# Two sets of halves of q and k, freer order of scores and transposes, in an attention and MLP kernel

## The chip, the cores and the metric

The kernel runs on one core of one Trainium2 chip. The metric is the device time of one execution, in microseconds (us). Three runs of the kernel before took 924.66, 919.51 and 918.96 us, a median of 919.51. The engines are named as in the profile: PE is TensorE (PEld its weight loads), DVE is VectorE, ACT is ScalarE, POOL is GpSimd, SP is SyncE, whose queue (SPq) issues nearly all transfers.

## The reference

Causal attention in blocks of 64 over q, k and v of shape (8 batches, 8 heads, 576, 64), and on its result, reshaped to 4608 tokens of 512, an MLP with 2048 hidden units and the activation h * tanh(softplus(h)):

```python
scores = scale * np.matmul(q, k.transpose(0, 1, 3, 2))
scores = np.where(block_i >= block_j, scores, -1000000000.0)   # blocks of 64
scores = scores - np.max(scores, axis=-1, keepdims=True)
attn = np.exp(scores)
attn = attn / (np.sum(attn, axis=-1, keepdims=True) + 1e-09)
out = np.matmul(attn, v)                # attention
...
h = x @ w_in                            # (4608, 512) @ (512, 2048)
sp = np.where(h > 20.0, h, np.log1p(np.exp(np.minimum(h, 20.0))))
y = (h * np.tanh(sp)) @ w_out           # (4608, 2048) @ (2048, 512)
```

All inputs and outputs are f32.

## The kernel before

Most products are made of pairs of f16 numbers: a matrix is split into a high half (the value in f16) and a low half (the rest), and a product is three matmuls, high by high, high by low, low by high. Scales that are powers of two, found from sums of squares, keep the halves in range.

The work is in tiles of 512 tokens. Tile b holds tokens of batch b, for b from 0 to 7; a ninth tile holds the 64 tokens that each batch has over 512. A tile has three stages: attention of the batch by pairs of heads (4 pairs), m1 (x by w_in, with the activation behind it) and m2 (by w_out, then the store). Attention of batch 0 has a form of its own (`attend`, L1345 to L1493, in f32). Batch 1 takes the scores in f32, and batches 2 to 7, 24 pairs, take them from halves (`attend_pair`). m1 is plain for the first tiles (L2156), then a scheme of seven products in place of eight (L2247); m2 is plain (L2596) up to tile 6 and by seven products after that (L2428). Attention of batch b runs beside m1 and m2 of the tile before it, so that PE always has matmuls that need nothing new.

A pair of batches 2 to 7 goes as follows. `load_pair` issues the loads of q and k into the f32 rooms `qf` and `kl`, and of v. ACT takes the sums of squares of both (L1173), and as it must write its squares somewhere, it writes them into the low halves QL and KL. A small matmul (L779) adds over the partitions, DVE makes the scales (L757, L767, L1185). Then the high halves QH and KH are made on ACT (L1213), DVE (L1217) or POOL (L792), and the low halves on DVE (L1225). There is one set of these four halves, so the squares of a pair must wait until PE has taken the scores of the pair before it (`wait_s`, with NQ = 1). The scores are three rounds in two banks of PSUM (`ss_ring`): L1563 for the products, each a pair of 64-row matmuls for the two heads of the pair, and L1575 for the columns that lie outside the mask: `far_q` times `far_k`, a constant tile of 64 columns of 2^120, adds a very large negative number. DVE takes the maxima (L1609 to L1619), ACT the exponentials (L1645), which are split in halves into a ring of three tiles P (cast on any of three engines, L1689; subtraction on DVE or POOL, L1696). SP transposes each by DMA into a ring of four tiles PT (L1724, and L1739 for a late piece). PE multiplies with v (L1779), DVE divides (L1845, L1846).

The program is a list of operations, each with what it needs (`after`), which ring rooms it takes and frees, and on which engines it can run. `Plan.order` lays them out with a table of due times, `AT` (one number for each operation), and a string, `WAY`, that names the engine of each operation that has a choice. In each engine the operations stand in the order so found, and each engine works strictly through its own list. The operations are given to the planner pair by pair. Besides the real needs two chains of needs are given: `last["S"]`, by which each round of scores comes after the round before it, over all pairs, and `last["T"]`, by which each transpose comes after the one before it.

Other lines that the prediction speaks of: the weight w_in comes in eight pieces of 1 MB (L853), each put together from its parts by a cast (L876) on ACT, DVE or POOL and an operation of DVE (L891); `far_q` columns for batch 0 (L1357, L1431); subtraction of the maxima for batch 0 on PE (L1459), which needs a scaled unit matrix from ACT (L810); casts of k and q for the maxima (`kr`, `qr`: L1297 on ACT, L1303 on DVE, L1308 on POOL); the exponentials of batch 0 (L1477); the activation (L2184 in the plain m1, L2300 in the other); the factors of the output (L1057) and the scaled output on ACT (L2637).

Of the kernel before, what the change touches and what calls it, by code (L numbers as in the profile page):

```python
# [12 lines left out]
BF16 = mybir.dt.bfloat16  # L13
F32 = mybir.dt.float32
# [7 lines left out]
P = 128  # L22
# [7 lines left out]
FULL = 1  # L30
EARLY = 6
SEVEN = 7
NWORK, NOT, NQ, NV, NPT, NP2 = 3, 1, 1, 1, 4, 3
# [2911 lines left out]
```

## Time and profile before

| what | value |
|---|---|
| median of three runs | 919.51 us (918.96 to 924.66) |
| profiled execution | 919.17 us, span of its instructions 917.4 us |
| PE, PEld busy | 908.8 us (99%), 636.6 us (69%) |
| DVE, ACT, POOL busy | 775.8 us (85%), 610.5 us (67%), 254.9 us (28%) |
| mean granted clock of PE | 1.000 |
| transfers | 129.94 MB, 142 GB/s |
| chain that ended last | PE 85%, DVE 6%, DMA 4%, ACT 2% |

The profile comes from the execution of 919.17 us. Busy time of an engine is the time in which at least one of its instructions runs; a PE instruction is shown up to the modelled end of its pipeline, so that consecutive matmuls overlap and their starts, not their lengths, tell the rate. In square brackets stands the idle time of the engine before an instruction, with what ended it. The chain of waits is followed back from the last instruction to what released each.

### The profile page before, as it was taken

The numbers are of one execution on the slowest core, as the hardware profiler recorded it, in microseconds if no ns is written. First come the engines' busy times: TensorE is split into PE (matmuls) and PEld (weight loads), VectorE is DVE, ScalarE is ACT, GpSimd is POOL, SyncE is SP. The second block draws the span as 40 slices with busy tenths as digits, with TensorE's granted clock in tenths as the row PEclk, the third lists the DMA queues.
The fourth block names the chain that finished last, engine by engine and source line by source line (L and its number), as shares of the span: only waits on it lengthen the run. The fifth ranks groups of instructions, "written<-read, shape, count | busy, mean of one in ns | idle before, by whom it ended". The sixth has DMA issues, their size and how long they took to land.

```text
span 917.4 us, 22914 instructions
## 1 busy us (share of the span) xinstructions
PE 908.8 (99%) x9288; PEld 636.6 (69%) x9288; DVE 775.8 (85%) x1466; ACT 610.5 (67%) x1043; POOL 254.9 (28%) x245
## 2 busy tenths in 40 slices
PE   8999999999999999999999999999999999999998
PEld 6976765555557865687557855785578757888887
DVE  6989999999989898698888887789778898984871
ACT  4789998799657974587569855677478433652540
POOL 2101221512245053343223341312614112300310
PEclk9999999999999999999999999999999999999999
DMA  9876997756798778867796588776877450015001
GB/s 304 263 227 155 214 242 158 142 125 153 153 192 175 150 145 181 157 128 152 156 200 140 110 176 176 162 135 125 178 135 138 77 112 14 1 52 111 2 1 47
DMA packets 298154, 129.94 MB, mean 142 GB/s; under 512 B 250944, under 2 KB 279616, under 8 KB 298048
## 3 DMA queue, kind: packets, MB, share of 16 engines
q1 hardware_dynamic: 297616, 128.16, 64.5%
q8 instruction: 72, 1.18, 0.5%
q10 hardware_dynamic: 432, 0.33, 0.1%
q14 instruction: 34, 0.28, 0.1%
HBM read 58.06 MB, written 10.49 MB: 75 GB/s over the span
## 4 chain that ended last, share of the span: by engine, by line
PE 85%; DVE 6%; DMA 4%; ACT 2%; SPq 1%; issue 1%; POOL 1%; DVEq 0%; POOLq 0%; ACTq 0%
PE acc L2247 28%; PE acc L2596 27%; PE ss L2428 8%; PE acc L2156 7%; PE ss L1563 7%; PE acc L1779 7%; DMA wo_l<-in_w_in_dram 2%; DVE P L1696 1%; DVE pv L1609 1%; DVE PT L1387 1%; DMA sx<-in_v_dram 1%; PE acc L1493 1%; DVE Gt L891 1%; DMA many<-in_k_dram 1%; DMA PT<-P 0%
## 5 line engine op out<-in xcount | busy, mean ns | idle before, releaser
L2596 PE MATMUL acc<-Gt,wo_h 128*128 128x512 f16 x896 | 266.7, 379 | 0.0
L2596 PE MATMUL acc<-Gt,wo_l 128*128 128x512 f16 x448 | 169.8, 379 | 0.0
L1645 ACT ACTIVATE pe<-ss,pv 128x192 f32<-128x192 f32 (+2 forms) x240 | 126.7, 608 | 60.5 <-DVE pv L1619 44.2
L2247 PE MATMUL acc<-x,wi_h 128*128 128x256 f16 x896 | 151.1, 273 | 0.0
L2596 PEld LDWEIGHTS <-wo_h 128*128 128x128 f16 x896 | 81.5, 98 | 86.1 <-issue 3.8
L2247 PE MATMUL acc<-x,wi_l 128*128 128x256 f16 x448 | 122.1, 273 | 0.0
L2247 PE MATMUL acc<-x,sx 128*128 128x256 f16 x1008 | 120.9, 273 | 0.0
L1609 DVE TENSOR_REDUCE pv<-ss 128x2 f32<-128x384 f32 (+4 forms) x140 | 104.5, 788 | 16.2 <-PE ss L1575 15.9
L2247 PEld LDWEIGHTS <-sx 128*128 128x128 f16 x1008 | 97.8, 98 | 14.4 <-issue 0.8
L2105 DVE SCALAR_TENSOR_TENSOR Gt<-F,bv,Gt 128x1024 f16<-128x1024 f32 (+2 forms) x80 | 95.4, 1203 | 3.5 <-POOL Gt L792 2.2
L2247 PEld LDWEIGHTS <-wi_h 128*128 128x128 f16 x896 | 86.3, 98 | 15.1 <-issue 1.1
L1696 POOL TENSOR_TENSOR P<-pe,P 128x256 f16<-128x256 f32 (+3 forms) x58 | 70.5, 1237 | 82.5 <-DVE P L1689 30.9
L2156 PE MATMUL acc<-x,wi_h 128*128 128x384 f16 (+2 forms) x384 | 80.5, 308 | 0.6 <-ACT F L2184 0.6
L2596 PEld LDWEIGHTS <-wo_l 128*128 128x128 f16 x448 | 43.8, 98 | 53.0
L1779 PEld LDWEIGHTS <-PT 128*128 128x128 f16 x2128 | 72.0, 97 | 9.2 <-issue 0.4
L2300 ACT ACTIVATE F<-acc,bv 128x512 f32<-128x512 f32 x84 | 57.0, 683 | 31.9 <-PE acc L2247 31.8
L1696 DVE TENSOR_TENSOR P<-pe,P 128x256 f16<-128x256 f32 (+3 forms) x110 | 73.9, 714 | 1.8 <-POOL P L1689 0.9
L1779 PE MATMUL acc<-many,PT 128*128 128x65 f16 (+1 forms) x2128 | 74.2, 193 | 0.0
L1563 PE MATMUL ss<-many 64*128 64x64 f16 (+7 forms) x1280 | 73.7, 260 | 0.0
L1689 POOL CAST P<-pe 128x256 f16<-128x256 f32 (+3 forms) x55 | 38.1, 717 | 90.8 <-ACT pe L1645 49.2
L2156 PE MATMUL acc<-x,wi_l 128*128 128x384 f16 (+2 forms) x192 | 56.0, 308 | 0.0
L1563 PEld LDWEIGHTS <-many 64*128 64x128 f16 x1152 | 33.6, 94 | 29.1 <-issue 14.8
(254 smaller groups left out, 1650.1 us busy)
## 6 DMA issues: line engine op xcount, KB each, us to landing
sx<-in_w_out_dram SPq DMA_DIRECT2D x16, 511.8 KB, 4.4
many<-in_v_dram SPq DMA_DIRECT2D x28, 288.0 KB, 3.2
many<-in_k_dram SPq DMA_DIRECT2D x28, 288.0 KB, 3.5
many<-in_q_dram SPq DMA_DIRECT2D x28, 256.0 KB, 3.5
out_dram<-ot SPq DMA_DIRECT2D x28, 256.0 KB, 2.8
wo_l<-in_w_in_dram SPq DMA_DIRECT2D x6, 1023.8 KB, 8.0
many<-in_v_dram SPq DMA_DIRECT2D x28, 192.0 KB, 3.4
many<-in_v_dram SPq DMA_DIRECT2D x28, 96.0 KB, 3.0
```

Of the source, the lines that this page charges most:

```text
L1563: nc.tensor.matmul(ss[:, 512 * a + col : 512 * a + col + n], lhsT=m[q_][hs, at : at + P], rhs=m[k_][hs, key : key + n], start=first, stop= ...
L1609: nc.vector.reduce_max(out=mx[:, c], in_=ss[:, :, c0:c1], axis=mybir.AxisListType.X)
L1645: nc.scalar.activation(pe[ex[r].slot][:, cols], ss_[S0[r].slot][:, cols], AF.Exp, scale=esc, bias=mx[:, c, a : a + 1],)
L1689: op(out=h, in_=x)
L1696: eng.tensor_sub(l, x, h)
L1779: nc.tensor.matmul(out, lhsT=p_, rhs=v_, start=first, stop=True, skip_group_check=True,)
L2105: nc.vector.scalar_tensor_tensor(out=dst[:, 1], in0=src, scalar=self.s_g, in1=dst[:, 0], op0=ALU.mult, op1=ALU.subtract,)
L2156: nc.tensor.matmul(pt, lhsT=w[:, d, f * P : (f + 1) * P], rhs=rhs(x, d), start=k == 0 and d == 0 and z == 0, stop=d == NP - 1 and z == 2, ...
L2247: nc.tensor.matmul(pt[:, k * TH : (k + 1) * TH], lhsT=weights(kind, z, d, k), rhs=x_[:, d, blk, x, :], start=first and k == 0 and d == 0 a ...
L2300: lambda: nc.scalar.activation(dst(), src(), AF.Mish, scale=scale),
L2428: nc.tensor.matmul(pt[:, k * TH : (k + 1) * TH], lhsT=weights(kind, z, s, c, k), rhs=block(blk, x, s, c), start=one, stop=s == NS - 1 and ...
L2596: nc.tensor.matmul(pt, lhsT=w[:, f, o * P : (o + 1) * P], rhs=g, start=s == 0 and c == 0 and z == 0, stop=s == NS - 1 and c == FG - 1 and ...
```

## The change

- There are two sets of halves QH, QL, KH, KL (`sets`, NQ = 2). Pair i of batches 1 to 7 uses set (i + 1) mod 2, and its squares and halves wait for the scores of the pair two before it, not one. The f32 rooms `qf` and `kl` stay single. The second set lies at the end of the tile `many`, which grows from 5632 to 6790 columns.
- To make room, small tiles are joined into one tile `small` (total, far_scale, pv, wv, dv), and `far_k` is no longer a tile of 64 columns: it is one column of `consts`, which the matmul reads 64 times (a broadcast).
- The chain of scores is given only for the first two of the pairs; later ones are ordered within a pair alone. The chain of transposes is gone (L1724 needs only its halves; the late piece L1739 still comes after its own).
- `AT` and `WAY` are new: another order on every engine, and other engines for many operations. No operation is added or removed but for the fills of constants.

```diff
-NWORK, NOT, NQ, NV, NPT, NP2 = 3, 1, 1, 1, 4, 3
+NWORK, NOT, NQ, NV, NPT, NP2 = 3, 1, 2, 1, 4, 3
 AT = (
-    0, 6736, 0, 475, 7565, 3975, 3325, 950, 1425, 10650, 4450, 2375, 1900, 5100, 5750, 6657, 8719,
...
+    0, 1050, 0, 475, 8745, 2850, 3325, 950, 1425, 1900, 5100, 3975, 2375, 8270, 10170, 9695, 7464,
...
 WAY = (
-    "dpdpaaaaaadaaaaadaaadadddppddapadapaaaaaaadppaaaddddadadaaadaaaaapapddaaaapddaaaddadddpdad"
+    "dddpaaaaaappaaaaaappdppaapdddpddaadaapddadpppadpddpdadadaaddaaaaadaapaadpaapaaaapapddpdad"
...
-    many = const.tile([P, 5632], F32, name="many")
+    many = const.tile([P, 5510 + 2 * S + P], F32, name="many")
...
+    small = const.tile([P, NPV * 19 + 2 * 33 + B // 2 + 1], F32, name="small")
...
+    def halves_in(q, k):
+        m = {}
+        for x, t in (("Q", q), ("K", k)):
+            t_ = t.rearrange("p (z n) -> p z n", z=2)
+            m.update({x + "H": t_[:, 0], x + "L": t_[:, 1], x + "F": t.bitcast(F32)})
+        return m
+
+    other = many_h[:, 11020 : 11020 + 4 * S + 2 * P]
+    sets = [
+        halves_in(qk[:, 2 * (S + P) : 4 * (S + P)], qk[:, 4 * (S + P) + 2 * S :]),
+        halves_in(other[:, 0 : 2 * (S + P)], other[:, 2 * (S + P) :]),
+    ]
...
-    far_k = const.tile([P, 64], BF16, name="far_k")
+    far_k = consts.bitcast(BF16)[:, 4:5]
     nc.vector.memset(far_k, 2.0**120)
+    far_k = far_k.to_broadcast([P, 64])
...
-        m = {**(fulls[i % 2] if full else sets[i % NQ]), **v_sets[i % NV]}
+        m = {**(fulls[i % 2] if full else sets[(i + 1) % NQ]), **v_sets[i % NV]}
...
-                S0.append(add("pe", (0.01, 0.0), lambda: None, [last.get("S")], take=[ss_ring]))
-                last["S"] = S0[r]
+                first = [last.get("S")] if len(used) < 2 else []
+                S0.append(add("pe", (0.01, 0.0), lambda: None, first + S0[-1:], take=[ss_ring]))
...
-                [lo, last.get("T")],
+                [lo],
                 take=[pt_ring],
                 free=[(p2_ring, hi)],
             )
-            last["T"] = tr
...
-            back = 2 if b <= FULL else NQ
-            wait_s = used[-back]["S"] if len(used) >= back else []
+            wait_s = used[-2]["S"] if len(used) >= 2 else []
```

How the new tables move instructions is shown at three places. In the changed program the lines are 4 to 5 higher (L1349 for L1345, L1463 for L1459, L814 for L810, L880 for L876, L1481 for L1477; 2 to 4 in the later ones: L1177 for L1173, L2186 for L2184, L1649 for L1645).

Place one, the start of the program. On ACT before, from its third row on (kr and qr are the casts of k and q of pair 1, PT is written with the scaled unit matrix):

```order
L1297 ACT_TABLE_LOAD
L1297 CAST kr_145<-sx_76 128x576
L1297 CAST qr_149<-sx_76 128x384
L810 ACTIVATE PT_107<-P_103 128x128
L1477 ACTIVATE pe_127<-ss_129 128x2x384
L1477 ACTIVATE pe_126<-ss_128 128x2x384
```

and in the change:

```order
L814 ACT_TABLE_LOAD
L814 ACTIVATE PT_105<-P_101 128x128
L1481 ACTIVATE pe_116<-ss_118 128x2x384
L1481 ACTIVATE pe_117<-ss_119 128x2x384
L1301 CAST kr_136<-wo_h 128x576
L1021 ACTIVATE P_100,bv_112<-sx_75 128x640
```

The unit matrix is first now, and the casts of pair 1 stand on POOL. On PE at the same place, before, where the scores of pair 0 end:

```order
L1431 LDWEIGHTS PT_107
L1431 MATMUL ss_129<-far_k,PT_107 128x64
L1459 LDWEIGHTS PT_106
L1459 MATMUL ss_129<-PT_107,PT_106 128x128
L1459 LDWEIGHTS PT_106
```

and in the change:

```order
L1435 LDWEIGHTS PT_105
L1435 MATMUL ss_119<-consts,PT_105 128x64
L1349 MATMUL acc_120<-kr_135,qr_139 128x384
L1349 MATMUL acc_121<-kr_135,qr_139 128x384
L1349 MATMUL acc_120<-kr_135,qr_139 128x128
```

The twelve subtractions L1459 stood right behind the scores; now the maxima products of pair 1 come between.

Place two, the last pieces of w_in. On ACT before (the cast of a piece, then the exponentials of batch 0):

```order
L1819 ACTIVATE dv_124<-acc_131,bv_118 128x4
L876 CAST Gt<-wo_l 128x1024
L1477 ACTIVATE pe_127<-ss_128 128x2x384
L1876 CAST P_102<-many 128x128
L876 CAST wo_l<-sx_76 128x8x64
```

and in the change on POOL:

```order
L880 CAST Gt<-x 128x1024
L1312 CAST qr_138<-wo_h 128x256
L1883 CAST x<-many 128x384 x3
L880 CAST Gt<-wo_l 128x1024 x2
L2828 MEMSET wo_l 128x8x64 x2
```

The last two casts of pieces into Gt have gone to POOL, and no exponential stands behind them.

Place three, m1 of tile 1. On ACT before (squares of q and k of the third pair of batch 2, then a load of the activation's table and two activations):

```order
L1645 ACTIVATE pe_126<-ss_128,pv_116 128x64
L1173 ACTIVATE many,pv_117<-many 128x576 x2
L2184 ACT_TABLE_LOAD
L2184 ACTIVATE F_65<-acc_130,bv_119 128x512
L2184 ACTIVATE F_65<-acc_132,bv_119 128x512
```

and in the change:

```order
L2186 ACT_TABLE_LOAD
L2186 ACTIVATE F_65<-acc_122,bv_113 128x512
L2186 ACTIVATE F_65<-acc_120,bv_113 128x512
L1177 ACTIVATE many,small<-many 128x576
L2095 ACTIVATE Gt<-F_65,bv_113 128x1024
```

One of the two squares has moved behind the two activations, the other stands well ahead of them.

## Rows read from the trace of the kernel before

**Rows 1.** The page, first part: busy time, share and instructions of each engine.
```profile
PE 908.8 (99%) x9288; PEld 636.6 (69%) x9288; DVE 775.8 (85%) x1466; ACT 610.5 (67%) x1043; POOL 254.9 (28%) x245
```

**Rows 2.** Stretches: length, busy PE, PEld, DVE, ACT, POOL, PE's clock, DMA share, GB/s.
```profile
0.00:20.00 20.00, 17.17 (x170) 12.87 (x170) 11.24 (x52) 9.81 (x19) 3.92 (x12) 1.00 0.91 286
900.00:920.00 20.00, 13.50 (x124) 11.84 (x122) 1.79 (x4) 1.31 (x3) 0.00 (x0) 0.99 0.16 53
```

**Rows 3.** Timeline, first 14 us: start, length, instruction, [idle before it, releaser].
```profile
7.56 0.67 ACT L1297 CAST kr<-sx 128x576 fp32r<-128x576 f32 x1 [4.61 <-DMA sx<-in_k_dram]
8.55 0.30 ACT L810 ACTIVATE PT<-P 128x128 f16<-128x128 f32 x1
8.91 0.83 PE L1459 MATMUL ss<-PT,PT 128*128 128x128 f16 x12 [1.69 <-ACT PT L810]
9.67 0.51 PE L1345 MATMUL acc<-kr,qr 64*128 64x384 f32 x4
...
13.03 0.51 POOL L1308 CAST qr<-wo_h 128x384 fp32r<-128x384 f32 x1 [9.90 <-DMA wo_h<-in_q_dram]
```

**Rows 4.** Timeline, 54 to 57 us.
```profile
54.13 1.35 ACT L876 CAST Gt<-wo_l 128x1024 f16<-128x1024 bf16 x1 [2.16 <-DMA wo_l<-in_w_in_dram]
...
56.20 1.09 PE L1420 MATMUL ss<-wo_h 64*128 64x192 f32 x12 [0.91 <-ACT pe L1477]
```

**Rows 5.** Timeline, 153 to 157 us.
```profile
153.17 2.34 DVE L970 SCALAR_TENSOR_TENSOR wo_l<-sx,wo_s,wo_h 128x2048 f16<-128x2048 f32 x1
...
155.68 0.69 ACT L2637 ACTIVATE ot<-acc,bv 128x512 f32<-128x512 f32 x1 [2.49 <-DVE bv L1057]
...
156.42 0.16 PE L779 MATMUL acc<-bv,consts 128*128 128x4 bf16 x1 [0.35 <-ACT ot L2637]
```

**Rows 6.** Timeline, 188 to 192 us.
```profile
188.28 0.68 ACT L1173 ACTIVATE many<-many 128x576 f16<-128x576 f32 x1 [0.59 <-DMA many<-in_k_dram]
...
189.07 1.28 ACT L2184 ACT_TABLE_LOAD   x1
...
191.10 0.59 PE L2156 MATMUL acc<-x,wi_h 128*128 128x512 f16 x2 [0.64 <-ACT F L2184]
```

**Rows 7.** Timeline, a change from 128-row to 64-row matmuls on PE.
```profile
103.31 0.28 PE L2156 MATMUL acc<-x,wi_h 128*128 128x128 f16 x2
103.42 0.22 PE L2156 MATMUL acc<-x,wi_l 128*128 128x128 f16 x1
103.57 1.26 PE L1563 MATMUL ss<-many 64*128 64x128 f32 x12
```

**Rows 8.** Timeline, first 4 us: a constant and the first matmuls, which read it.
```profile
0.31 0.10 POOL L2917 MEMSET const-bfloat16-1.0<- 128x1 bf16 x1
...
0.77 2.72 PE L730 MATMUL acc<-const-bfloat16-1.0 128*128 128x512 bf16 x6 [0.77 <-PEq L2917]
```

**Rows 9.** Groups by line and shape, count | busy us, mean ns | idle before, releasers.
```profile
L1575 PE MATMUL ss<-far_k,far_q 64*128 64x64 bf16 x168 | 11.7, 190 | 0.0
...
L1173 ACT ACTIVATE many<-many 128x576 f16<-128x576 f32 x48 | 32.6, 679 | 26.7 <-PE ss L1563 19.1 <-DMA many<-in_k_dram 6.9 <-DMA many<-in_q_dram 0.6
...
L1696 DVE TENSOR_TENSOR P<-pe,P 128x768 f16<-128x768 f32 x22 | 21.1, 957 | 0.0
...
L1696 POOL TENSOR_TENSOR P<-pe,P 128x768 f16<-128x768 f32 x6 | 10.5, 1748 | 18.8 <-ACT P L1689 14.2 <-issue 4.6
```

**Rows 10.** Timeline, DVE's low halves beside POOL at 471 us, and alone at 567 us.
```profile
471.17 3.92 DVE L1225 SCALAR_TENSOR_TENSOR many<-many,pv 128x704 f16<-128x704 f32 x2
471.77 2.71 POOL L1696 TENSOR_TENSOR P<-pe,P 128x1024 f16<-128x1024 f32 x1
...
475.44 0.84 PE L1563 MATMUL ss<-many 64*128 64x128 f16 x18
...
567.82 0.81 DVE L1225 SCALAR_TENSOR_TENSOR many<-many,pv 128x576 f16<-128x576 f32 x1
```

**Rows 11.** The waits of SP's queue: for whom, us in total, times, longest.
```profile
SPq L1724 <- PE acc L1779: 12.0, 6, 3.2
```

More of the change, by code (lines that the diff above doesn't have):

```diff
@@ L324 @@
 WAY = (
-    "dpdpaaaaaadaaaaadaaadadddppddapadapaaaaaaadppaaaddddadadaaadaaaaapapddaaaapddaaaddadddpdad"
-    "pdpaddpadadaadadadddaadadadaaadaddaaaapaaaapddppddaddpdddddadddpapppdpdpdddddaddpddddddpdd"
-    "dpdddapdpdadpdpdppdddddpdaadadpdadddpapadadpdadddpdddpaaaaddddpdapddadadadddddpddadadaaaaa"
-    "dadddadadaapddadaaaappapdpadddpappdppaddddddpddadppadpdadpaappappdaaaddppdpaaaadaadapadddp"
-    "ddaadaaadadpdpdppdaddpdddapdpdaapddpadaapdppdppdappapdaddpaapddddaddaddpdaapdaadpaddappaaa"
-    "aadaadddadadpappdadapaapddddapdpaapadpdadapdappdadaddddddapaaapaaadpddaapdaadpaaaadapappad"
-    "ddaappapdpddddaadddpaddappppddddadpaadadpdddpddppdpaadpddadapaaddddaaadaaaapdaddapppdapaap"
-    "dadpddadddpdadapapdapapaadpdappddddaadddpaddddddpdppdddddddaddddadddadddadpdpppdddaddddddd"
-    "dpdddadpddadpdadddappddadddaddddpdaadaaadddaapaaaaaadddapdpaaaaadddaadaaaaaaddadadddddpadd"
-    "adpdpadadaddddpdaapaaadddpppaadaadpddpappdaaaddddaadadaaaadda"
+    "dddpaaaaaappaaaaaappdppaapdddpddaadaapddadpppadpddpdadadaaddaaaaadaapaadpaapaaaaapapddpdad"
+    "pdppdpdaaadaadadaddaaadadaddaadaadaapdadaddpdddddpapddaddpdppdddpdpdadddddppdaddppaddpaddd"
+    "ddddpdpdpdappdapdppppdpadaadadadapddaaaadapadddaddppddaaadpddadaaadaadadapaaadppdpdaaddpaa"
+    "dppaddpdaaappdaaaaaappadadddapaadapppdaadddpapappdpppapaappdppapaddaaddpdpddadadaaaaddaaad"
+    "daaddddadapppdpdadaaapapddpapddppdddadppadpppddadddaddadadadddpdpapdadapaadpaaadpddaapadaa"
+    "dpaaapddadaadppaddpddddppdddadapdappdpdaaappppapadaddppppdddaaaadddpadadppadaddadddadapppp"
+    "dddapaaadapapaadpddpadapaapdpppadpppdpadpddaapddpddaddpddadppaadaaaaapaaaaadddpdppadaaappa"
+    "dapapdapddddaddpapdadddadpddapdpdddaaddddaddppdpddaddpdddddadpdpadddadddadpdpadddpddddadpp"
+    "addpdadddpddddadddppdddapdadddpaadappdaadddpdpdaaaaadddaapppadaadddaadaaaadadaadddaddddppd"
+    "addddpdaaddddppdpapaaaddpaadappadddddppppadaaadddaadaaaadaaaa"
 )
@@ L620, in attention_moe @@
     left = dram.tile([P, NP, B // 2, P], F32, name="left")
-    far_scale = const.tile([P, B // 2], F32, name="far_scale")
-    total = const.tile([P, 1], F32, name="total")
+    NPV, NBV = 4, 3
+    small = const.tile([P, NPV * 19 + 2 * 33 + B // 2 + 1], F32, name="small")
+    pv = [small[:, i * 19 : (i + 1) * 19] for i in range(NPV)]
+    small = small[:, NPV * 19 :]
+    wv = [small[:, i * 20 : (i + 1) * 20].rearrange("p (a n) -> p a n", a=5) for i in range(2)]
+    dv = [small[:, 40 + i * 13 : 53 + i * 13] for i in range(2)]
+    far_scale, total = small[:, 66 : 66 + B // 2], small[:, 66 + B // 2 :]
     KW = 640
@@ L669, in attention_moe @@
     qk = many_h[:, 4096 : 4096 + 8 * S + 4 * P]
-    m, at = {}, 0
-    for x, n in (("Q", S + P), ("K", S)):
-        for full in (True, False):
-            t = qk[:, at : at + 2 * n]
-            at += 2 * n
-            if full:
-                m[x] = t.bitcast(F32)
-            else:
-                t_ = t.rearrange("p (z n) -> p z n", z=2)
-                m.update({x + "H": t_[:, 0], x + "L": t_[:, 1], x + "F": t.bitcast(F32)})
-    qf, kl = m["Q"], m["K"]
-    sets = [m]
-    consts = const.tile([P, 2], F32, name="consts")
+    qf, kl = (t.bitcast(F32) for t in (qk[:, 0 : 2 * (S + P)], qk[:, 4 * (S + P) : 4 * (S + P) + 2 * S]))
+    def halves_in(q, k):
[9 more added lines that the diff above has]
+    ]
+    consts = const.tile([P, 4], F32, name="consts")
     full_esc, one = consts[:, 0:1], consts.bitcast(BF16)[:, 2:3]
@@ L715, in room @@
         return [const.tile(shape, dt, name=f"{nm}{i}") for i in range(n)]
-    NPV, NBV = 4, 3
-    pv = room(NPV, "pv", [P, 19])
     bv = room(NBV, "bv", [P, 24])
-    wv = room(2, "wv", [P, 5, NG])
-    dv = room(2, "dv", [P, 13])
     wmax = dv[0][:, 12:13]
@@ L1748, in attend_pair @@
                 tr.free, tr.frees = [], []
-                last["T"] = late
         st["ends"] += ex
```

562 rows, old and new, of the table AT are left out of this document.

## The prediction

> **What bounds the kernel now.** I read the busy shares first. PE is busy for 908.8 us of 917.4, every other engine for 85% or less [rows 1]. DVE, the next, has some 140 us to spare over the span. So the time is PE's list of matmuls, and a change can win only PE's idle time, or the time its instructions take.
>
> Then the stretches and the timeline of PE. The idle time, 8.6 us, is at few places. The first 20 us have 2.83 us (20.00 less 17.17) [rows 2]: 0.77 before the first matmul [rows 8], 1.69 before the subtraction of the maxima L1459, which waits for the scaled unit matrix of L810 on ACT [rows 3], and the rest for the first loads. At 56 us PE waits 0.91 us for an exponential L1477 [rows 4], at 156 us 0.35 us for an output tile on ACT [rows 5], at 191 us 0.64 us for the activation [rows 6]. The last 20 us show PE idle for 6.50 us in a stretch of which the span covers 17.4 [rows 2]: 3.9 us are the last division and store, which the change does not touch. Add: 2.83 + 0.91 + 0.35 + 0.64 + 3.9 = 8.6. Nothing is left over: in batches 2 to 7, where the two sets of halves are used, PE never waits for scores, halves or transposes.
>
> The third view is the groups of instructions. The wait that the second set takes away exists: ACT stood idle for 19.1 us before the squares L1173, ended by scores of PE [rows 9]. But that is ACT, busy for 67%, and no wait of PE ends on it in the stretches above, except in part at 191 us.
>
> **The change part by part**, against the profiled execution of 919.17 us (its span 917.4 and some 1.8 around it; the median of the runs shown is 919.51, 0.34 above it).
>
> *The second set.* The squares of a pair no longer need the scores of the pair just before. That may take up to 19.1 us of idle time from ACT [rows 9] and gives DVE and ACT more freedom; on PE's path it is worth 0, since PE's waits there are 0. The cover is PE's own list; were PE to catch up with the halves anywhere, the second set would then be worth something, which no row shows.
>
> *The start.* L810 was queued behind the casts kr and qr on ACT, of which kr itself waited 4.61 us for its load until 7.56 [rows 3]. Now it is first on ACT, and the casts are on POOL; PE takes the maxima products of pair 1 (L1345) ahead of L1459. What is late next is the cast: in_k lands at about 7.5; POOL takes 0.51 us for 384 columns [rows 3], so an estimated 0.77 for kr's 576. If the cast of q is done by then, L1345 starts at about 8.4; if both come after the load, at 8.9, as PE does now (8.91 [rows 3]). The gain is 0 to 0.5 us. **−0.3**, in the middle.
>
> *56 us.* The exponential stood behind a cast of a weight piece on ACT, which waited 2.16 us for its load and took 1.35 [rows 4]. That cast and one other are on POOL now, and nothing that PE needs soon is behind them; in POOL's list the cast of q of pair 1 stands between them, and POOL is busy for 28% [rows 1]. **−0.9**, the whole wait; at worst 0, if the exponential is then late for another reason.
>
> *156 us.* The factors (L1057) still stand behind the operation L970 of 2.34 us on DVE [rows 5], and the small matmul waits for a bank that comes free after them. **0**; between −0.35 and 0.35.
>
> *191 us.* The activation was behind two squares on ACT, the first of which waited 0.59 us for its load and took 0.68 [rows 6]. One of the two is behind the activations now, the other well ahead. The table load of 1.28 us can then begin earlier. **−0.6**; at worst 0.
>
> *Far columns.* The constant is read 64 times over from one column. The nearest row is the first six matmuls, which read a constant of 128x1 as 512 columns, 2.72 us for six [rows 8], 0.45 us each with the pipeline's end. The twelve matmuls of 128 columns in rows 3 take 0.83 us, by which 512 columns would take 0.28. So the repeated column is slower there by a factor of up to two, or PE itself was slower in its first microseconds: 512 columns at the lower of its two levels, 1.2 GHz, are 0.43 us, which fits, though the granted clock in the stretch reads 1.00 [rows 2]. If it is the column, a 64-column matmul costs 64/2.4 = 27 ns more; the 168 of later batches run side by side in pairs for two heads [rows 9], 84 x 0.027 = 2.3 us, with those of batch 0 (fewer than half as many) about 3. I take **0**, since the factor agrees to a few per cent with that of the clock's levels, and keep +3 as a rival. The smaller fill of the constant is on POOL in the first microsecond, hidden.
>
> *Scores and transposes without chains, new order.* PE has the same matmuls. Its list has 71 runs of 64-row matmuls where it had 75; a change of rows costs about 0.1 us (0.15 from the last 128-row start to the first 64-row one, against 0.05 to 0.06 between matmuls of 128 columns [rows 7]), so **−0.4**, 0 to −0.4. The transposes now go in whatever order rooms of PT come free; the listing has more of them (53, from 27) behind a matmul of PE. On SP's queue such a wait exists, six of them, 12.0 us together, the longest 3.2 [rows 11]; what is queued behind are loads and the transposes of other pairs, and PE's product with v (L1779) waits for the transposes. None of the six holds PE. Whether a new one does can't be read from the trace. From below, the waits of the new order are 0; from above, as much as the old order had in the middle, 0.91 + 0.35 + 0.64 = 1.9. I take half, **+0.9**: the waits of the old order are the only rows there are, and the new one is freer.
>
> *Casts and subtractions between engines.* Of the subtractions L1696 of 768 columns eight move from DVE (957 ns) to POOL (1748 ns) [rows 9]: −7.7 us on DVE, +14.0 on POOL. Altogether POOL has 295 instructions for 250 and DVE 1420 for 1468 in the lists. Neither is near full, so 0 on the path; their price if the cover is gone is a rival below.
>
> Sum: −0.3 − 0.9 − 0.6 − 0.4 + 0.9 = −1.3, so 919.17 − 1.3 = **917.9 us**. With the bounds: best −0.5 − 0.9 − 0.6 − 0.4 − 0.35 = −2.75, 916.4; worst, with the credits but the whole 1.9 of new waits and nothing for start and switches, +0.4, 919.6. Its own range is 916.4 to 919.2, above which it is the first rival.
>
> **The rivals.**
>
> *The new order has as many waits of its own as it removes, or a little more.* Same mechanism as the old waits: an engine's list with a late operation ahead of one that PE needs. For it: 26 more transposes are tied to PE, and one wait of the size of rows 11 that reaches PE is up to 3.2 us. Against it: PE has 99% and nothing in batches 2 to 7 was late before, and now less is tied. Time: 919.2, between 918.8 and 920.5.
>
> *Repeated columns at half rate.* Price above: 917.9 + 3 = 920.9. For it the first six matmuls; against it that the factor is the clock's.
>
> *POOL's subtractions hold DVE (slower than before).* Two low halves L1225 of 704 columns took 3.92 us at 471 us beside a subtraction on POOL, where one of 576 columns alone took 0.81 [rows 10], by columns 0.99 for each, 1.98 for both: 1.94 us lost, beside 2.71 us of POOL. DVE ended at 475.09 and the scores began at 475.44: 0.35 us were left [rows 10]. The Trainium skill, "GPSIMD Engine Reference", section 1 (Specifications), says that GpSimd shares its SBUF interfaces with VectorE, in contention with instructions of two SBUF inputs, which low halves and subtractions are; the trace agrees at this place. By that rule every subtraction that goes to POOL costs DVE something; the busy time of DVE would fall by less than the moved work. By the rows: eight more of 768 columns, each costing up to 1.94 x 768/1024 = 1.45 us, less the 0.35 of slack, 1.1. If four fall on low halves for which PE waits, 4.4 us: 922.3; all eight, 926.7. It decides where low halves end less than a microsecond before their scores. Against it: DVE sheds 7.7 us, and with two sets the halves can be made a whole pair ahead, so that the slack grows.
>
> *All waits go, the one at 156 us too, and no new one comes.* 919.17 − 0.5 − 0.9 − 0.35 − 0.6 − 0.4 = 916.4, and with the first loads a bit earlier 915.8: little below it is possible, since PE's own work, the start and the tail make 915.2 (919.17 less 3.6 of waits and 0.4 of changes of rows).
>
> **How the numbers follow.** Chances: the forecast 0.57, as many new waits 0.23, half rate 0.05, POOL against DVE 0.08, no wait left 0.07. The range from 915.8 to 921.2 takes in the forecast, the first rival and the last, most of the second and little of the third: some 0.9 by the cases, and about 0.8 after a deduction, since my estimate of what the new order waits for is from one row. Less than 1%, 9.2 us, cannot be told from no change here; faster than 910 is below what PE's list allows, 0.01; slower than 928.7 needs more than the far end of the third rival, 0.03; within 1% 0.96.
>
> **What the profile of the changed kernel would show.** PE's busy time within 1 us of 908.8. The start: no idle time of a microsecond before the subtraction (now L1463), and PE idle in the first 20 us down from 2.83 to about 2.5. No wait of 0.91 at 56 us and none of 0.64 at 191 us; the 0.35 at 156 us still there. The squares (now L1177) no longer with idle time ended by PE's scores, and yet no faster kernel for it. Far columns with a mean near 190 ns as before; some 27 ns more would show the half rate. DVE's busy time down by 8 us or more (48 instructions fewer) if the moved work is free, less if POOL holds it; POOL's up by 14 or more. I would be wrong by a mechanism that I did not see if PE shows waits over 1 us in batches 2 to 7, on a transpose or on low halves, or if its matmuls themselves take another time for the same shapes.

## The result, and the profile after

The changed kernel takes 926.59 us (median of 18 runs, 924.36 to 929.85), the kernel before 918.72 in as many runs: ratio 1.0077, interval 1.0062 to 1.0091. By the ratio it is slower by 5.7 to 8.4 us (by the medians 7.9), clear of noise, and outside of the range. In 27 of 114 later runs of the kernel before, and in none of 77 with the new order, PE's mean granted clock was below 0.998 and the time some 5 us longer; "at full clock" below means the median of the other runs.

The page of the changed kernel, its first part, against [rows 1]:

```profile
span 925.9 us, 22919 instructions
PE 911.0 (98%) x9288; PEld 637.8 (69%) x9288; DVE 762.2 (82%) x1418; ACT 608.8 (66%) x1044; POOL 299.5 (32%) x290
```

DVE sheds 13.6 us and POOL gets 44.6 more, and PE's matmuls are the same; the span is 8.5 us longer. The longest of PE's waits (engine, line and operand, what it waited for; us in total, times, longest):

```profile
PE ss L1567 <- ACT pe L1649: 3.0, 4, 1.2
PE acc L2249 <- DVE many L1848: 1.2, 2, 0.8
PE acc L783 <- DVE ot L2627: 0.9, 1, 0.9
...
PE acc L2158 <- DVE many L1848: 0.6, 1, 0.6
PE ss L1349 <- DVE PT L1391: 0.5, 1, 0.5
PE acc L1781 <- DVE many L1229: 0.5, 1, 0.5
```

None of these stands in the kernel before. The sum by stretch (length, then busy PE, PEld, DVE, ACT, POOL, clock, DMA share, GB/s), first of the kernel before, then of the changed one:

```profile
20.00:80.00 60.00, 59.09 (x580) 48.29 (x575) 56.52 (x126) 49.37 (x77) 5.47 (x7) 1.00 0.75 241
80.00:320.00 240.00, 239.00 (x2486) 146.48 (x2485) 225.10 (x437) 197.89 (x336) 73.39 (x65) 1.00 0.80 169
320.00:660.00 340.00, 340.00 (x3698) 227.41 (x3696) 287.25 (x542) 232.17 (x424) 117.72 (x114) 1.00 0.77 154
```

```profile
0.00:20.00 20.00, 18.56 (x180) 13.71 (x181) 11.08 (x52) 8.50 (x15) 4.21 (x12) 1.00 0.92 292
20.00:80.00 60.00, 58.66 (x573) 48.92 (x571) 56.95 (x123) 50.60 (x77) 14.72 (x16) 1.00 0.75 239
80.00:320.00 240.00, 234.53 (x2435) 141.91 (x2434) 222.16 (x409) 192.72 (x335) 78.03 (x72) 1.00 0.77 166
320.00:660.00 340.00, 337.60 (x3681) 227.68 (x3680) 276.06 (x528) 234.34 (x420) 129.52 (x130) 1.00 0.75 153
```

The first 20 us lose 1.44 us of PE where they lost 2.83 [rows 2]: a gain of 1.4. But from 20 to 80 us PE is idle for 1.34 us against 0.91, from 80 to 320 us for 5.47 against 1.00, and from 320 to 660 us for 2.40 against 0. All stretches together are 5.9 us more of idle time (the tail after the last matmul, 0.3 more, apart). The other 2.3 us are in PE's busy time (911.0 for 908.8): where a wait begins, the matmul ahead of it is shown up to its modelled end, some 0.1 us of each wait. The starts of the matmuls, which do not hang on modelled ends, agree: the pauses of more than 0.08 us beyond the usual distance of two such matmuls sum to 28.2 us for 19.8, 96 of them for 75. So the whole loss is waits of PE, twenty or so of 0.1 to 1.2 us.

### The profile page after: what moved, and what is told of

It is laid out like the page before. It is cut to its first block, busy times and chain, and to the rows that moved or that the text cites. A ratio compares the mean times of both kernels' runs of the same rounds, so it can differ in the third digit from the quotient of the medians.

```text
span 925.9 us, 22919 instructions
## 1 busy us (share of the span) xinstructions
PE 911.0 (98%) x9288; PEld 637.8 (69%) x9288; DVE 762.2 (82%) x1418; ACT 608.8 (66%) x1044; POOL 299.5 (32%) x290
## 4 chain that ended last, share of the span: by engine, by line
PE 67%; DVE 19%; ACT 6%; DMA 5%; issue 3%; SPq 1%; POOL 0%; DVEq 0%; ACTq 0%
PE acc L2249 24%; PE acc L2598 22%; PE ss L2430 8%; PE acc L1781 5%; PE ss L1567 4%; PE acc L2158 4%; DVE small L1613 3%; DVE P L1700 2%; ACT pe L1649 2%; DVE Gt L2107 1%; DVE many L1229 1%; DMA PT<-P 1%; DVE PT L1391 1%; DMA wo_l<-in_w_in_dram 1%; DVE wo_l L974 1%
## 5 line engine op out<-in xcount | busy, mean ns | idle before, releaser
L1649 ACT ACTIVATE pe<-ss,small 128x192 f32<-128x192 f32 (+2 forms) x240 | 126.7, 608 | 55.2 <-DVE small L1623 33.8
L1700 POOL TENSOR_TENSOR P<-pe,P 128x512 f16<-128x512 f32 (+3 forms) x78 | 88.2, 1154 | 89.3 <-ACT P L1693 36.8
L1613 DVE TENSOR_REDUCE small<-ss 128x2 f32<-128x384 f32 (+4 forms) x140 | 104.3, 787 | 11.6 <-PE ss L1579 11.5
L2107 DVE SCALAR_TENSOR_TENSOR Gt<-F,bv,Gt 128x1024 f16<-128x1024 f32 (+2 forms) x80 | 98.9, 1244 | 10.7 <-POOL Gt L796 5.3
L1700 DVE TENSOR_TENSOR P<-pe,P 128x256 f16<-128x256 f32 (+3 forms) x90 | 66.9, 780 | 3.1 <-ACT P L1693 2.2
L1693 ACT CAST P<-pe 128x256 f16<-128x256 f32 (+3 forms) x87 | 50.7, 636 | 9.5 <-DMA PT<-P 5.4
```

The lines of the kernel that those rows point to most:

```text
L1613: nc.vector.reduce_max(out=mx[:, c], in_=ss[:, :, c0:c1], axis=mybir.AxisListType.X)
L1649: nc.scalar.activation(pe[ex[r].slot][:, cols], ss_[S0[r].slot][:, cols], AF.Exp, scale=esc, bias=mx[:, c, a : a + 1],)
L1693: op(out=h, in_=x)
L1700: eng.tensor_sub(l, x, h)
L2107: nc.vector.scalar_tensor_tensor(out=dst[:, 1], in0=src, scalar=self.s_g, in1=dst[:, 0], op0=ALU.mult, op1=ALU.subtract,)
```

## The experiments

Two theories came out of the traces. **W**: the SP queue waits where it did not before. Its own waits have a new row (the queue of the changed kernel), which the kernel before lacks:

```profile
SPq L1158 <- DMA many<-in_v_dram: 10.3, 6, 2.5
```

A load of v waits for another load of v to land. **H**: subtractions on POOL hold DVE's small operations on the way from scores to exponentials. The rivals: the second set, the repeated column or the missing chains cost time by themselves; or the new order is too tight without either.

**1. The old tables in the changed program.**

```diff
 # the changed kernel, with AT and WAY of the kernel before
-AT, WAY = (new)
+AT, WAY = (old)
```

> The changed program with the old AT and WAY: two sets of halves, the repeated far column and no chains stay, the order and the engines go back (nearly: without the chains a few operations around 400 and 475 us come to stand in another place). Theory 1 (the new order brings the waits, the other parts of the change cost nothing): 918 to 921 us, PE idle near 5 us, no wait over 0.5 us between 60 and 350 us but those at 156 and 191 us that the kernel before had, far columns at the same pitch. Rival 2 (the second set, the repeated column or the missing chains cost time by themselves, by the column's reads or by halves in another place): 924 to 927 us.

Measured: 923.39 us, ratio 1.0053 (1.0033 to 1.0074), between the two ranges; at full clock 923.19 for 918.77. Theory 1 falls: with the old order, which came out the same as before on every engine, instruction for instruction but for the fills and one load of a table, 4 to 5 us are lost all the same. Its trace can be laid beside that of before instruction by instruction, and that showed W. First the kernel with the old tables, around 140 us:

```profile
138.00 1.20 SPq L1742 DMA_TRANSPOSE many<-P  x1
139.98 0.68 ACT L1177 ACTIVATE many<-many 128x576 f16<-128x576 f32 x1 [0.97 <-DMA many<-in_q_dram]
140.10 1.25 SPq L1158 DMA_DIRECT2D many<-in_v_dram  x2
144.22 0.53 SPq L1138 DMA_DIRECT2D many<-in_k_dram  x1
147.61 0.68 ACT L1177 ACTIVATE many<-many 128x576 f16<-128x576 f32 x1 [1.44 <-DMA many<-in_k_dram]
148.43 0.16 PE L783 MATMUL acc<-small,consts 128*128 128x2 bf16 x1 [1.00 <-ACT many L1177]
```

Then the kernel before at the same place:

```profile
136.88 1.19 SPq L1739 DMA_TRANSPOSE many<-P  x1
138.12 1.26 SPq L1154 DMA_DIRECT2D many<-in_v_dram  x2
141.60 1.01 SPq L1134 DMA_DIRECT2D many<-in_k_dram  x1
145.64 0.68 ACT L1173 ACTIVATE many<-many 128x576 f16<-128x576 f32 x1
```

Before, the loads of v go out right behind the transpose (138.12 after 136.88 + 1.19). Now 0.9 us pass (140.10 after 138.00 + 1.20), and all behind them on the queue is late. Counted from the transpose, which itself starts 1.1 us later, the load of k is late by 1.5 us and its square on ACT by 0.9 (by the clock 2.6 and 2.0), and PE waits 1.00 us for the sum that comes from the squares.

In the built program the two differ in the waits that SP's instructions carry. Four loads bring v of a pair into its room `VL` in `many`; one (64x2x128) goes to rows 3 and 5 of the room, and one (64x128) to row 4, between them. At 6790 columns the row 4 load waits for the other one, as if the two overlapped; at 5632 it does not. Rows of SP's list of the changed kernel (DMAHW with a number is a transfer that must have landed), and of the same with two columns more:

```
L1158 DMA many<-in_v_dram 64x128 [waits DMAHW2_49,DMAHW1_49]     many: 6790 columns
L1158 DMA many<-in_v_dram 64x128 [waits DMAHW1_49]               many: 6792 columns
```

Building with other widths showed the pattern for this wait: 5632, 5636, 5640, 6792, 6796 and 6800 are free of it, 5633, 5634, 5638, 5646, 6790 and 6794, which are no multiples of 4, have it. In the changed kernel it stands in 25 of 28 places. It is not the only wait that goes by the width (experiment 3).

**2. The width alone**, in three kernels:

```diff
 # the changed kernel (x_w6792), and the same with the old tables (x_oldtab6792)
-    many = const.tile([P, 5510 + 2 * S + P], F32, name="many")
+    many = const.tile([P, 5512 + 2 * S + P], F32, name="many")
 # the kernel before (n_w5634)
-    many = const.tile([P, 5632], F32, name="many")
+    many = const.tile([P, 5634], F32, name="many")
```

> The kernel before with one edit: `many` has 5634 columns, not 5632, two more that nothing uses. Its SP queue gets the waits of the changed kernel with the old tables, one for one; the order on every engine and all else is the same. Theory W: 922 to 925 us, slower by 0.4 to 0.7%, with waits of PE at about 148, 250, 300 and 676 us. Rival: no change, 918 to 919.5 us.

Measured: 924.22 us, 1.0048 (1.0024 to 1.0072); at full clock 923.70 for 918.22. Two unused columns cost the kernel before 2.2 to 6.6 us, with nothing else changed; its waits for L1154 on a load of v are 20.1 us on SP. That the width costs time is shown here. That all of it comes by the load of v is not: the same two columns bring a second kind of wait, on DVE (experiment 3).

> The changed kernel with one edit: the tile `many` has 6792 columns, not 6790. Every engine has the same instructions in the same order. What goes is a wait on SP's queue: at 6790 columns one load of v (64x128, row 4 of the room) waits for the landing of the load just before it (rows 3 and 5), since the two strided regions are taken to overlap; at 6792 (a multiple of 4) they are not, in 25 of 28 places. Theory W (that wait holds SP's queue for 1 to 3 us at a time, loads and transposes behind it land later than the order allows for, and PE waits): PE's waits from 100 us on fall from 7.6 to 2 us or less, 917 to 920 us. Rival R (the new order is too tight by itself): 924 to 927 us as before the edit.

Measured: 924.52 us, 1.0056 (1.0038 to 1.0074), 2.1 us less than the changed kernel. The time lies in the rival's range, and PE's idle time from 80 to 320 us is still 3.44 us (5.47 before the edit; the profiled execution is one of the faster ones, 922.99 us). So W is part of it, not the most.

> The changed program with the old AT and WAY (the run of that before was 923.4 us) and `many` at 6792 columns. Its SP queue has the waits of the kernel before, one for one, and every engine its order. Left of the change: the second set, the repeated far column, the joined small tiles. Theory W: 918 to 919.5 us, within 0.1% of the kernel before, since neither the second set nor the far column costs or gives PE anything. Rival 2 (one of these costs time by itself): 922 us or more.

Measured: 921.91 us, 1.0033 (1.0011 to 1.0055); at full clock 921.21 for 918.22. 1.5 us of the 4.6 go (at full clock 1.4 of 4.4); what is left fits neither figure.

**3. What the rest of the program costs in the old order.** One set in use, and the far column alone in the kernel before:

```diff
 # x_old_oneset: old tables, 6792 columns
-        m = {**(fulls[i % 2] if full else sets[(i + 1) % NQ]), **v_sets[i % NV]}
+        m = {**(fulls[i % 2] if full else sets[0]), **v_sets[i % NV]}
...
-            wait_s = used[-2]["S"] if len(used) >= 2 else []
+            back = 2 if b <= FULL else 1
+            wait_s = used[-back]["S"] if len(used) >= back else []
 # n_far: the kernel before
-    consts = const.tile([P, 2], F32, name="consts")
+    consts = const.tile([P, 4], F32, name="consts")
...
-    far_k = const.tile([P, 64], BF16, name="far_k")
-    nc.vector.memset(far_k, 2.0**120)
+    far_k = consts.bitcast(BF16)[:, 4:5]
+    nc.vector.memset(far_k, 2.0**120)
+    far_k = far_k.to_broadcast([P, 64])
```

> The changed program with the old tables, `many` at 6792 columns, and one set of halves in use (all pairs take the first set, and the squares wait for the scores of the pair before): on every engine the order and the number of waits of the kernel before. Left of the change: the place of the tiles in memory, the joined small tiles and the repeated column. If the second set is what still cost 3 us in the run with the old tables and 6792 columns (921.9 us): 918 to 919.5 us. If the rest of the layout does it: 921 to 923 us.

> The kernel before with the far column alone: `far_k` is one column of `consts`, read 64 times; order, engines and waits are those of before. If a repeated column is read at full rate: the far matmuls stay at a mean of 190 ns and the time is 918 to 919.5 us. If at half rate: 217 ns and 921 to 922 us.

Measured: 920.69 us, 1.0011 (0.9990 to 1.0033), and 921.55 us, 1.0019 (0.9992 to 1.0047). By the ratios neither can be told from the kernel before, nor clearly from the 1.0033 of the run with both sets. At full clock the far column (919.54 for 918.72, six runs) still can't, but the run with one set can: 920.24 for 918.72, and all its nine runs are above that.

The traces have a candidate for this rest, which I did not look for. In x_oldtab6792 and x_old_oneset some divisions (L1848) wait for a transfer `left<-many`. DVE's waits for it, first in x_oldtab6792, then in the kernel before, and one of the places in both:

```profile
DVE many L1848 <- DMA left<-many: 5.3, 4, 2.5
DVE many L1846 <- DMA left<-many: 0.9, 2, 0.4
...
237.51 0.56 DVE L1848 TENSOR_TENSOR many<-acc,small 128x384 f32<-128x384 f32 x1 [2.13 <-DMA left<-many]
235.98 0.56 DVE L1846 TENSOR_TENSOR many<-acc,dv 128x384 f32<-128x384 f32 x1
```

The total is 6.7 us with one set, 5.9 in n_w5634 and 0.8 in n_far. The wait of 2.13 us stands on the chain to PE's wait of 0.63 us at 248 us, which the kernel before lacks. In the built programs the same eight waits of DVE differ from the kernel before at 5634, 6790 and 6792 columns; with one set at 6800 columns none differs, on any engine. So 6792 was no clean test of the width: it frees the loads of v and not these divisions. No run was made at 6800, so whether the second set costs anything in the old order stays open, and what the divisions cost is not shown. The far matmuls settle the column. The group in n_far:

```profile
L1576 PE MATMUL ss<-consts,far_q 64*128 64x64 bf16 x168 | 11.7, 190 | 0.0
```

190 ns, 11.7 us, to the digit the group of [rows 9]: a repeated column is read at full rate.

**4. POOL's subtractions.** In the changed kernel, from the third pair of batch 1 on, they do only half of their columns, so that the kernel leaves out the other half of these low halves; then the same at 6792 columns:

```diff
-            def rest(eng, pieces=pieces):
+            def rest(eng, pieces=pieces, part=1 + (len(used) >= 2)):
                 def emit():
                     for h, l, x in pieces():
-                        eng.tensor_sub(l, x, h)
+                        n = x.shape[-1] // (part if eng is nc.gpsimd else 1)
+                        eng.tensor_sub(l[..., 0:n], x[..., 0:n], h[..., 0:n])
```

> The changed kernel, but from the third pair of batch 1 on the subtractions L1700 that stand on POOL do only half of their columns (the other half of these low halves is left out); the order on every engine is the same. Theory H (POOL's two-input operations hold DVE, DVE sets the pace between 80 and 310 us, and the exponentials and so PE are late by it): the time DVE is held falls by half, PE's waits between 80 and 640 us fall from 7.5 to 3 us or less, 920 to 922 us. Rival R (the order stands too tight by itself, waits are for DMA, ACT and DVE's own work): less than 1.5 us better, 925 us or more.

> The changed kernel with both edits: `many` at 6792 columns (924.5 us alone) and half of the columns in POOL's subtractions L1700 from the third pair of batch 1 on (924.7 us alone, in the tile of 6790; their other half is left out). If the two causes add (the wait of SP on the load of v, 2.1 us, and POOL holding DVE, 1.9 us): 922 to 923 us. If it is one cause seen twice: 924 to 925 us.

Measured: 924.74 us, 1.0053 (1.0038 to 1.0068), and 922.74, 1.0024 (1.0007 to 1.0040). Halving alone gives 1.9 us, between what H and its rival had foretold, but the two edits add, as expected of two causes: 2.1 and 1.9 alone, 3.9 together. In the trace with the halving the waits between 258 and 281 us fall from 2.1 to 0.8 us, and those at 583 and 593 us go. But they are gone in the trace of x_w6792 too, which has no halving, so the times carry this experiment and not the places.

**5. The same load in the old order**: eight letters of WAY from `d` to `p`, for the first eight subtractions of 768 columns.

```diff
 # WAY of the kernel before, at eight operations L1696 (85 to 250 us)
-d d d d d d d d
+p p p p p p p p
```

> The kernel before with one edit: the first eight subtractions L1696 of the kind with 768 columns (batch 1 and 2, 85 to 250 us) move from DVE to POOL, in the old order. Theory H: DVE is held by more than it sheds where the maxima and low halves are due, PE gets waits of 3 to 15 us in all between 80 and 310 us: 922 to 934 us. Rival R (POOL's load matters little, the new order's own places of operations do it): below 920.5 us.

Measured: 922.66 us, 1.0042 (1.0023 to 1.0062), 2.1 to 5.7 us more (at full clock 921.80 for 918.77), with new waits of PE of 0.34, 0.68 and 0.54 us between 127 and 155 us in the profiled execution, the fastest (920.15 us). The moved work alone, without any new table of times, makes waits.

**6. One operation at a time**, in the changed kernel with 6792 columns. These two kernels have their tables on fewer lines, so that their line numbers are 290 lower (L1333 for L1623, L1330 for L1620, L1331 for L1621, L1410 for L1700).

```diff
 # x_w_104: WAY, the cast L880 at 96.65 us
-d
+a
 # x_w_rep: besides, the subtractions at 575 and 585 us, and AT of the second
-p p    582023
+d d    583100
```

The place of the first, in the run before it (x_w6792), DVE beside POOL:

```profile
95.42 1.30 DVE L1693 CAST P<-pe 128x256 f16<-128x256 f32 x3
95.85 2.70 POOL L1700 TENSOR_TENSOR P<-pe,P 128x256 f16<-128x256 f32 x3 [6.13 <-DVE P L1693]
96.65 1.41 DVE L880 CAST wo_l<-sx 128x512 f16<-128x512 bf16 x1
97.95 2.40 DVE L1613 TENSOR_REDUCE small<-ss 128x2 f32<-128x896 f32 x3
```

The cast takes 1.41 us and ends with POOL's work to within half a microsecond; in the kernel before its like took 0.45 at 100.51 us, where POOL was idle. The maxima L1613 begin that much later, and PE waits 1.22 us for the exponentials behind them.

> The changed kernel with `many` at 6792 columns and one operation on another engine: the cast L880 of 128x512 at 96.65 us, which took 1.41 us on DVE beside three subtractions on POOL (0.45 in the kernel before), goes to ACT. Behind it on DVE stand the maxima of a round, then the exponentials for which PE waits 1.22 us at 104 us. If POOL's hold on DVE makes that wait: it falls below 0.5 us, and the time by about 0.8 us. If the order does (exponentials late for another reason): the wait stays at 1.0 us or more.

Measured: 923.08 us, 1.0025 (1.0005 to 1.0045). The wait at 104 us is gone altogether, and the median falls by 1.4 us.

The second place, in the trace of x_w_104:

```profile
575.24 2.13 POOL L1410 TENSOR_TENSOR P<-pe,P 128x1024 f16<-128x1024 f32 x1 [1.03 <-ACT P L1403]
575.45 1.95 DVE L1333 TENSOR_SCALAR small<-small 128x4 f32<-128x4 f32 x1
...
585.08 2.41 POOL L1410 TENSOR_TENSOR P<-pe,P 128x256 f16<-128x256 f32 x3 [7.71 <-ACT P L1403]
585.77 1.11 DVE L1330 TENSOR_TENSOR small<-small 64x2 f32<-64x2 f32 x1
586.91 0.60 DVE L1331 COPY small<-small 64x2 f32<-64x2 f32 x1
```

> The run before (`many` at 6792 columns, one cast at 96 us on ACT: 923.1 us), and two more operations moved: the subtractions L1700 of 1024 columns at 575 us and of 256, 512 and 256 columns at 585 us go from POOL to DVE, the second behind the scaled maxima and the output tile. Beside them on POOL, DVE's small operations of the maxima took 1.95 us for 0.23 (at 575 us) and 1.11 and 0.60 for 0.17 each (at 586 us), and PE waited 0.62 us at 578 and 0.89 us at 588 us. If POOL's hold on DVE makes these waits: both fall to 0.3 us or less, 921.5 to 922.3 us. If the lists are too tight there for another reason: waits as before or longer, as DVE has 2.5 us more work, 923 us or more.

Measured: 922.01 us, 1.0021 (1.0001 to 1.0042). The same operations with POOL's work moved:

```profile
575.88 0.23 DVE L1333 TENSOR_SCALAR small<-small 128x4 f32<-128x4 f32 x1
...
584.49 0.16 DVE L1330 TENSOR_TENSOR small<-small 64x2 f32<-64x2 f32 x1
584.68 0.17 DVE L1331 COPY small<-small 64x2 f32<-64x2 f32 x1
```

Both waits of PE (0.62 and 0.89 us) are gone, though DVE has more to do: an operation of 128x4 had stood for nearly as long as POOL's subtraction, 1.95 us against 2.13. The median fell by 1.1 us, as far as expected. (The trace of x_w6792 lacks both waits without this edit, see Open; what shows the cause is the median and the lengths of the small operations.)

**7. The old waits, mended in the old order.**

```diff
-    0, 6736, 0, 475, 7565, 3975, ...
+    0, 5000, 0, 475, 7565, 3975, ...
-    "dpdpaaaaaadaaaaa...
+    "dpdpaaaaaadpaaaa...
```

> The kernel before with two edits of its tables alone: the scaled unit matrix (L810) stands ahead of the casts on ACT, and the cast of the weight piece at 52 us is made on POOL, not ACT. Tests the terms of the sum for the start and for 56 us: if they are right, the wait of 1.69 us before L1459 falls to 0 to 1 us and that of 0.91 us at 56 us goes, 916.5 to 917.5 us against 918.7. Rival (what is late next takes their place): 918.2 to 919.

Measured: 918.32 us, 0.9981 (0.9965 to 0.9996). By the ratio it is faster than the kernel before by 0.4 to 3.2 us; but the medians differ by 0.5 us (918.32 for 918.78, at full clock 918.77), which is in the rival's range. In its trace the subtraction of the maxima comes at 7.04 us (at 8.91 in [rows 3]) after a wait of 0.16 us, and the scores at 55 us without one:

```profile
7.04 0.84 PE L1169 MATMUL ss<-PT,PT 128*128 128x128 f16 x12 [0.16 <-DVE PT L1103]
...
54.94 0.98 PE L1130 MATMUL ss<-wo_h 64*128 64x192 f32 x12
```

That the edit took these waits away, the trace alone does not show. They differ between executions of the old order: the first 20 us cost PE 2.83 us in the trace of before, but 1.68 in x_oldtab, 1.88 in n_far and 1.23 in n_pool8, all with the unit matrix behind the casts; here they cost 1.53.

## Why the prediction was wrong

**The step that failed** is the term "+0.9" for the waits of the new order, with its upper end of 1.9. It was bounded by the waits that the old order had; the new one has 7.9 us of them from 80 us on (5.47 + 2.40). Two things were behind that, and the sum had neither.

- *A step that was costed at nothing.* That the tile `many` grows from 5632 to 6790 columns stood in the change, and I took only its contents into account. It puts a wait on SP's queue in 25 places. The rule "each queue that a step is moved past" was applied to transposes and not to the loads of v. It is about 2 us in the changed kernel (926.6 to 924.5), without the divisions that 6792 columns do not free, and 2.2 to 6.6 us in the kernel before (experiment 2). The lists of waits of the two programs, which could be compared ahead of the run, show it.
- *A rival at the wrong place, with too small a chance.* "POOL's subtractions hold DVE" was given 0.08, and 922.3 us. The mechanism was right; experiments 4 to 6 show it: 1.9 us by the halving, 2.5 us by the three moved pieces of work (924.5 to 922.0; two of the three are among the halved ones, so that the two figures are not to be added). But I looked for it at the low halves (L1225), where the second set gives slack, and there the mean of 128x704 did fall, from 1125 to 945 ns. It sat on the small operations behind the maxima, L1620 and L1623, whose forms of 64x2 and 128x4 rose from a mean of 228 to 298 and of 282 to 386 ns (128x6 fell, from 282 to 246), and on DVE's casts. Scores, maxima, exponentials are a chain on which nothing can be made ahead. The trace of before had that price too (the operation took 0.85 us at 106 us beside POOL); I took the one row with the longest time and not the rows on the chain that PE waits for. The rule of the Trainium skill ("GPSIMD Engine Reference", section 1, Specifications) names DVE instructions of two SBUF inputs and those in a 2-port mode; I weighed the first half alone. The held operation of 128x4 and the held cast have one tensor input each; whether they ran in such a mode, no run here shows.

**What held.** The start: the wait of 1.69 us before L1459 went, and PE lost 1.44 us in the first 20 us, a gain of 1.4 for which I had at most 0.5, since the load of k landed at 7.1 and not at 7.5, and a cast on POOL took 0.67 us, not 0.77. That size is partly luck of the two executions: over all traces the old order at the start loses 1.23 to 2.86 us there, the new one 1.20 to 1.50. The row of the changed kernel:

```profile
7.83 0.50 PE L1349 MATMUL acc<-kr,qr 64*128 64x384 f32 x4 [0.20 <-POOL kr L1312]
8.34 0.84 PE L1463 MATMUL ss<-PT,PT 128*128 128x128 f16 x12
```

At 56 us the wait fell only from 0.91 to 0.51, as another took its place (L1349 for DVE at 55.42 us). The wait of 0.64 us at 191 us is gone; that of 0.35 at 156 us went too, where I had kept it, and one of 0.48 us for a low half came at 160 us. The second set did what it says, ACT no longer waits for PE before the squares, and it gave PE nothing:

```profile
L1177 ACT ACTIVATE many<-many 128x576 f16<-128x576 f32 x48 | 32.7, 684 | 23.9 <-DMA many<-in_k_dram 18.0 <-DMA many<-in_q_dram 5.8
```

Against [rows 9]: of 26.7 us of idle time 23.9 are left, now for the loads of k and q (6.9 and 0.6 before). The wait moved from PE to the loads, whose f32 rooms are still single: the queue's loads of q and k wait for the low halves that read them (SPq L1138 <- DVE many L1229, 14.3 us in nine waits). The repeated column costs nothing, as taken. DVE's time fell by 13.6 us, where 8 or more was foretold; what its instructions took beyond the median of their form without POOL beside them, summed over those with POOL beside them, rose from 37.4 to about 44 us, and between 50 and 300 us from 10.6 to 20.2. The −0.4 for fewer changes of rows was not tried alone, and no run shows it.

**Open.** Of the 7.9 us between the medians, 6792 columns and the three pieces of work moved account for 4.6 (926.6 to 922.0). What remains, 1.9 us by the ratio of x_w_rep (0.1 to 3.9) and 3.6 at full clock (922.01 for 918.41), beside a start that is no worse, are waits like these in x_w_rep (line numbers 290 lower): 0.59 us at 108 and 0.48 at 159, each behind a small DVE operation of 128x4 that stood beside one on POOL (0.83 and 1.07 us; the first beside a scaling of one tensor, no subtraction), which was read and not tried, and 1.13 us at 418 us, behind a division that waited for a transfer:

```profile
PE acc L1959 <- DVE many L1558: 1.1, 1, 1.1
...
PE acc L1868 <- DVE many L1558: 0.6, 1, 0.6
...
417.13 0.56 DVE L1558 TENSOR_TENSOR many<-acc,small 128x384 f32<-128x384 f32 x1 [1.82 <-DMA left<-many]
```

This last wait goes by the width too: in the built programs of the changed order the division carries it at 6790 and 6792 columns and not at 6800. So the width's share is probably more than the 2 us that 6792 columns gave back; no run at 6800 shows how much.

The missing chains could not be tried alone: the new order uses the freedom. Nor could the new tables be run with one set. And some waits, as that at 593 us, stand in the profile of one kernel (the changed one, x_w_104) and not of its neighbour (x_w6792) with the same order: where a subtraction on POOL meets a small operation on DVE differs between executions.

## What to carry to other kernels

When one engine is busy for 99%, a change has little to win and a new order much to lose: bound the waits of a new order by the slack of its chains, not by the waits of the old one. Compare the waits of the two built programs on every queue and every engine, also where only the size of a tile changed, and do so again for the mended one. Put work on POOL, two-input subtractions above all, where DVE has no short operation on the way from PE to PE.

## What was not expected of the hardware

DVE operations of a few columns can last nearly as long as the POOL instruction beside them: 128x4 took 1.95 us for 0.23, a cast of 128x512 1.41 for 0.45, while POOL's subtraction of 1024 columns ran (2.13 us) or three of 256 to 512 (2.70 us). A matmul's moving operand may be one column repeated 64 times, at the same 190 ns. And two columns more in a tile of 5632 cost 0.48% (0.24 to 0.72), by waits that the program then carries.

PE's clock can fall too. In the trace of n_w5634 it did so in the stretch in which PE waited 0.32 and 1.04 us, between 55 and 57 us, and was then at the lower level, 1.2 GHz (stretches as above, the clock third from the end):

```profile
50.00:55.00 5.00, 4.72 (x46) 3.70 (x42) 4.40 (x10) 1.17 (x4) 0.00 (x0) 1.00 1.00 344
55.00:60.00 5.00, 3.92 (x25) 3.52 (x25) 3.96 (x10) 3.98 (x7) 0.98 (x2) 0.61 0.30 86
60.00:65.00 5.00, 5.00 (x30) 4.20 (x31) 2.31 (x8) 2.45 (x6) 0.00 (x0) 0.50 0.73 212
```

In the trace of the kernel before, with 0.91 us at the same place [rows 4], the clock stayed at 1.00. Why the one fell and the other did not, and whether the new order is what spares it the fall, no run here shows.
